# Reading a weight matrix as the moving matmul operand in runs of 8 tokens instead of single strided tokens or a reordered copy

## The chip, the cores and the metric

One core of one Trainium2 chip. The metric is the device time of one execution in microseconds (us), the median of several runs. In this kernel TensorE (PE in the profile) multiplies matrices: one operand, `lhsT`, is loaded first (PEld in the profile, whose page counts 4826 loads for 4826 matmuls), the other, `rhs`, is the moving operand. Operands lie in the memory called SBUF, results in the one called PSUM. VectorE (DVE) and ScalarE (ACT) move results out of PSUM, GpSimd (POOL) prepares the next batch and issues loads.

## The reference

The input `x` is 8 batches of 3008 tokens with 256 features. A two-dimensional Fourier transform is followed by an MLP-mixer block:

```python
X = np.fft.fft(np.fft.fft(x, axis=1), axis=2)
x = X.real
xt = x.transpose(0, 2, 1)
h = np.maximum(xt @ w_tok1, 0.0) @ w_tok2          # w_tok2: 256 x 3008
u = x + h.transpose(0, 2, 1)                       # "the add into u"
h2 = np.maximum(u @ w_ch1, 0.0) @ w_ch2            # 256 -> 1536 -> 256
return u + h2
```

The change touches only the second product of the token mixer, `... @ w_tok2` ("tok2"), and the add into `u`.

## The kernel before: the parts that matter

The kernel factors 3008 as 64 x 47: token `t = 47*b + a`. The Fourier tables leave the tokens of `u` ordered "k2-major": all 64 values of `b` for the first `a`, then for the next `a`, and so on. `w_tok2` lies in SBUF (`w2s`, 16-bit floats) in natural order, so tokens that are neighbours in k2-major order lie 47 elements, or 94 bytes, apart.

The token axis is cut in six chunks of 512 columns (eight `a`, the last one seven: 448 columns). For each chunk and each half `h` of the features, two matmuls add into one PSUM tile `pu`, and DVE adds `yt`, the Fourier part:

```python
w2p = const.tile([P, 2, S], FP16, tag="w2p")

def w2_cols(c):
    a0, a1 = 8 * c, min(8 * c + 8, NQ)                       # NQ = 47
    return w2s[:].rearrange("p h (b a) -> p h a b", a=NQ)[:, :, a0:a1, :]

def order_w2(c, th):                                         # ACT makes the copy
    a0, a1 = 8 * c, min(8 * c + 8, NQ)
    out_ = w2p[:, th, 64 * a0:64 * a1].rearrange("p (a b) -> p a b", b=64)
    copy(0, out_, w2_cols(c)[:, th])
# ... (in the generator `front(b)`, which makes u of batch b) ...
for c in range(NCH):                                         # 6 chunks
    f0 = CW * c
    n = min(CW, S - f0)
    for h in range(2):
        pu = ps_f("pu")                                      # PSUM, 3 buffers
        for th in range(2):
            nc.tensor.matmul(pu[:, 0:n], lhsT=uu[:, th, int(minus), h, :],
                             rhs=(w2_cols(c)[:, th] if b == 0 else
                                  w2p[:, th, f0:f0 + n]), ...)
        # ... y = the piece of yt, forwards or mirrored ...
        nc.vector.tensor_tensor(out=ut[:, h, f0:f0 + n], in0=pu[:, 0:n],
                                in1=y, op=AT.add)
```

Batch 0 cannot wait for the copy and reads `w2s` with the stride. In batch 0 ACT also makes the copy `w2p`, which batches 1 to 7 read contiguously. The rest of TensorE's work is the channel mixer: `pc` (`u @ w_ch1`) and `po` (`@ w_ch2`). `front(b+1)` is woven between the `pc` and `po` groups of batch `b`.

## Time and profile before

Median 672.84 us of 3 runs (672.61 to 676.21).

| | before |
|---|---|
| PE busy, share of the span | 647.4 us, 96% |
| DVE / ACT busy | 333.5 / 327.5 us |
| 24 tok2 matmuls of batch 0 (stride of 94 bytes), 512 columns | 1409 ns each |
| 168 tok2 matmuls of batches 1 to 7 (contiguous), 512 columns | 379 ns each |
| first tok2 matmul of batch 0 / of batch 1 / last of batch 7 | 41.1 / 137.4 / 596.1 us |

First the page: busy time by engine, and the chain of work that ended last.

```profile
span 672.3 us, 11899 instructions
PE 647.4 (96%) x4826; PEld 431.8 (64%) x4826; DVE 333.5 (50%) x726; ACT 327.5 (49%) x671; POOL 244.6 (36%) x242
...
PE 93%; POOL 2%; DVE 2%; ACT 2%; issue 1%; DVEq 0%; POOLq 0%; ACTq 0%
```

TensorE is the limit. The windows view gives, for each stretch of time, the busy time of PE, PEld (the weight loads), DVE, ACT and POOL, then the granted TensorE clock, the share of DMA time and GB/s:

```profile
40.00:60.00 20.00, 18.90 (x38) 4.56 (x38) 7.76 (x14) 5.10 (x9) 12.15 (x10) 0.66 0.53 113
225.00:300.00 75.00, 75.00 (x590) 52.13 (x588) 38.03 (x82) 37.06 (x81) 31.24 (x27) 1.00 0.46 85
```

In the steady part TensorE has no idle time at all, so what is added to a matmul is paid. Early in batch 0 its granted clock is 0.66, two thirds of full.

The groups by line and form, for tok2 and its two companions (the columns: busy us, mean ns of one | idle time of the engine before them, and what ended it):

```profile
L509 DVE TENSOR_TENSOR ut<-pu,yt 128x512 f16<-128x512 f32 x80 | 52.3, 680 | 44.6 <-PE pu L500 44.6
L500 PE MATMUL pu<-w2p,uu 128*128 128x512 f16 x140 | 37.8, 379 | 0.2 <-DVE ut L509 0.2
L500 PE MATMUL pu<-w2s,uu 128*128 128x512 f16 x20 | 26.0, 1409 | 0.3 <-ACT qs L485 0.3
L291 ACT ACTIVATE w2p<-w2s 128x512 f16<-128x512 f16 x10 | 14.3, 1433 | 0.0
```

The tile view of tok2 has the first and last starts:

```profile
L500 PE MATMUL pu<-w2s,uu x24: 1232/1402/1424, 41.1 to 125.5; 128*128 128x512 f16 x20, 128*128 128x448 f16 x4
L500 PE MATMUL pu<-w2p,uu x168: 350/379/379, 137.4 to 596.1; 128*128 128x512 f16 x140, 128*128 128x448 f16 x28
```

A matmul's mean is its duration from start to end; in a row, they overlap (contiguous ones are 379 ns long and start 215 ns apart). The cost is the distance from one start to the next. The timeline of PE shows it (start, length, then the instructions that were merged):

```profile
70.06 2.62 PE L500 MATMUL pu<-w2s,uu 128*128 128x512 f16 x2
72.48 1.49 PE L532 MATMUL pc<-ut,wc1p 128*128 128x512 f16 x6
...
106.99 2.76 PE L532 MATMUL pc<-ut,wc1m 128*128 128x512 f16 x6
...
211.12 0.59 PE L500 MATMUL pu<-w2p,uu 128*128 128x512 f16 x2
211.55 1.30 PE L532 MATMUL pc<-ut,wc1m 128*128 128x448 f16 x6
```

Two strided matmuls hold TensorE from 70.06 to 72.48: 1.21 us each, about 2.4 ns a column. Two contiguous ones hold it from 211.12 to 211.55: 0.215 us each. At 106.99, six `pc` matmuls take nearly twice their usual time (2.76 us, where six take 1.49 at 72.48): the granted clock has fallen to half again (0.50 from 107.0 to 109.7 us, 1.00 from 70.0 to 72.5).

### The profile page before, as it was taken

The numbers are of one execution on the slowest core, as the hardware profiler recorded it, in microseconds if no ns is written. First come the engines' busy times: TensorE is split into PE (matmuls) and PEld (weight loads), VectorE is DVE, ScalarE is ACT, GpSimd is POOL, SyncE is SP. The second block draws the span as 40 slices with busy tenths as digits, with TensorE's granted clock in tenths as the row PEclk, the third lists the DMA queues.
The fourth block names the chain that finished last, engine by engine and source line by source line (L and its number), as shares of the span: only waits on it lengthen the run. The fifth ranks groups of instructions, "written<-read, shape, count | busy, mean of one in ns | idle before, by whom it ended". The sixth has DMA issues, their size and how long they took to land.

```text
span 672.3 us, 11899 instructions
## 1 busy us (share of the span) xinstructions
PE 647.4 (96%) x4826; PEld 431.8 (64%) x4826; DVE 333.5 (50%) x726; ACT 327.5 (49%) x671; POOL 244.6 (36%) x242
## 2 busy tenths in 40 slices
PE   4789999999999999999999999999999999999996
PEld 3533454666776767667766677666766677666665
DVE  8743332473366435654366435653366435654342
ACT  6625674426553565336543555346553655334341
POOL 8829729624930096204930096205800000000000
PEclk9878998999999999999999999999999999999999
DMA  9991541734292235725292336622241332232432
GB/s 154 172 193 35 100 96 39 99 82 71 48 155 68 64 81 101 100 55 85 55 166 50 63 91 107 85 70 68 48 92 35 63 91 48 48 79 60 95 78 60
DMA packets 86486, 56.27 MB, mean 84 GB/s; under 512 B 54768, under 2 KB 83376, under 8 KB 85680
## 3 DMA queue, kind: packets, MB, share of 16 engines
q1 hardware_dynamic: 78176, 38.04, 27.4%
q0 software_dynamic: 8256, 17.49, 16.4%
q8 instruction: 37, 0.61, 0.4%
q14 instruction: 17, 0.14, 0.1%
HBM read 34.98 MB, written 24.64 MB: 89 GB/s over the span
## 4 chain that ended last, share of the span: by engine, by line
PE 93%; POOL 2%; DVE 2%; ACT 2%; issue 1%; DVEq 0%; POOLq 0%; ACTq 0%
PE po L551 37%; PE pc L532 37%; PE pu L500 9%; PE pw L443 2%; PE pz L416 1%; PE pw L444 1%; PE py L482 1%; PE pq L482 1%; DVE ut L509 0%; ACT uu L474 0%; PE pz L432 0%; PE ph L363 0%; DVE osb L565 0%; POOL xm L118 0%; PE pz L426 0%
## 5 line engine op out<-in xcount | busy, mean ns | idle before, releaser
L532 PE MATMUL pc<-ut,wc1p 128*128 128x512 f16 x576 | 143.3, 385 | 0.4 <-DVE ut L509 0.4
L532 PE MATMUL pc<-ut,wc1m 128*128 128x512 f16 (+1 forms) x576 | 136.2, 373 | 0.0
L565 DVE TENSOR_TENSOR osb<-po,rt 128x254 f32<-128x254 f32 (+6 forms) x264 | 77.2, 346 | 59.1 <-PE po L551 54.7
L532 PEld LDWEIGHTS <-wc1p 128*128 128x128 f16 x576 | 53.9, 99 | 65.2 <-issue 20.0
L399 POOL TENSOR_TENSOR eo<-xp 94x512 f16<-94x512 f16 (+1 forms) x28 | 33.9, 1211 | 165.3 <-PE pz L432 164.1
L532 PEld LDWEIGHTS <-wc1m 128*128 128x128 f16 x576 | 55.1, 98 | 54.4 <-issue 1.1
L509 DVE TENSOR_TENSOR ut<-pu,yt 128x512 f16<-128x512 f32 (+1 forms) x96 | 61.6, 670 | 56.4 <-PE pu L500 56.4
L394 POOL TENSOR_TENSOR xd<-xp,xm 94x1024 f16<-94x1024 f16 x28 | 59.3, 2119 | 64.4 <-DMA xm<-in_x_dram,ix_76 64.4
L395 POOL TENSOR_TENSOR xp<-xp,xm 94x1024 f16<-94x1024 f16 x28 | 59.3, 2120 | 2.2
L291 ACT ACTIVATE w<-pw 128x259 f16<-128x259 f32 x90 | 30.1, 386 | 53.3 <-PE pw L444 52.7
L291 ACT ACTIVATE z<-pz 128x480 f16<-128x480 f32 (+1 forms) x59 | 34.3, 662 | 26.3 <-PE pz L416 19.4
L500 PE MATMUL pu<-w2p,uu 128*128 128x512 f16 (+1 forms) x168 | 44.2, 375 | 0.5 <-DVE ut L509 0.5
L487 DVE TENSOR_TENSOR yt<-py,qs 128x512 f16<-128x512 f32 x48 | 30.6, 686 | 19.5 <-ACT qs L485 9.7
L403 POOL TENSOR_TENSOR eo<-xd 94x508 f16<-94x508 f16 (+1 forms) x28 | 33.7, 1203 | 0.0
L500 PE MATMUL pu<-w2s,uu 128*128 128x512 f16 (+1 forms) x24 | 30.7, 1383 | 0.3 <-ACT qs L485 0.3
L500 PEld LDWEIGHTS <-uu 128*128 128x128 f16 x192 | 19.0, 99 | 13.1 <-issue 4.4
L485 ACT ACTIVATE qs<-pq 128x512 f32<-128x512 f32 x24 | 14.1, 596 | 19.4 <-PE pq L482 8.9
L443 PE MATMUL pw<-td_305,z 128*128 128x259 f16 x96 | 21.7, 277 | 0.9 <-ACT w L291 0.6
L444 PE MATMUL pw<-td_304,z 128*128 128x131 f16 x96 | 19.0, 223 | 0.0
L474 ACT ACTIVATE uu<-uv 128x256 f16<-128x256 f32 (+2 forms) x48 | 13.2, 337 | 9.9 <-DVE uv L469 9.9
L128 POOL DMA_DIRECT2D xp<-in_x_dram x32 | 17.2, 560 | 0.2 <-issue 0.2
L118 POOL DMA_INDIRECT xm<-in_x_dram,ix_76 x16 | 15.3, 955 | 4.7 <-issue 4.6
(420 smaller groups left out, 1136.8 us busy)
## 6 DMA issues: line engine op xcount, KB each, us to landing
out_dram<-osb SPq DMA_DIRECT2D x88, 256.0 KB, 3.3
xp<-in_x_dram POOLq DMA_DIRECT2D x16, 272.0 KB
xp<-in_x_dram POOLq DMA_DIRECT2D x16, 127.5 KB
rt<-ut SPq DMA_TRANSPOSE x96, 3.3
out_dram<-osb SPq DMA_DIRECT2D x8, 192.0 KB, 3.2
w2s<-in_moe_w_tok_dram POOLq DMA_DIRECT2D x1, 1504.0 KB
w1p<-in_moe_w_tok_dram POOLq DMA_DIRECT2D x2, 384.0 KB
wc_148<-in_moe_w_ch_dram POOLq DMA_DIRECT2D x1, 768.0 KB
```

Source lines behind the costliest of these rows:

```text
L291: nc.scalar.activation(out=out_, in_=in_, func=AFT.Copy)
L394: eng.tensor_tensor(out=xd[:, t, :], in0=xp[:, t, :], in1=rv, op=AT.subtract)
L395: eng.tensor_tensor(out=xp[:, t, :], in0=xp[:, t, :], in1=rv, op=AT.add)
L399: eng.tensor_tensor(out=eo[:, t, 1:129], in0=xp[:, t, 1:129], in1=xp[:, t, 255:127:-1], op=AT.add)
L403: eng.tensor_tensor(out=eo[:, t, 129:256], in0=xd[:, t, 1:128], in1=xd[:, t, 255:128:-1], op=AT.subtract)
L443: nc.tensor.matmul(pw[:, 0:WD], lhsT=zb, rhs=td1[:], start=True, stop=False)
L487: nc.vector.tensor_tensor(out=yt[:, h, CW * c:CW * c + CW], in0=py[:], in1=qs[:], op=op)
L500: nc.tensor.matmul(pu[:, 0:n], lhsT=uu[:, th, int(minus), h, :], rhs=(w2_cols(c)[:, th] if b == 0 else w2p[:, th, f0:f0 + n]), start=(th = ...
L509: nc.vector.tensor_tensor(out=ut[:, h, f0:f0 + n], in0=pu[:, 0:n], in1=y, op=AT.add)
L532: nc.tensor.matmul(pc[:, 0:n], lhsT=wc[:, h, ct * P:(ct + 1) * P], rhs=ut[:, h, f0:f0 + n], start=(h == 0), stop=(h == 1))
L551: nc.tensor.matmul(po[0:n, o:o + D], lhsT=c1[:, ct, ks * P:ks * P + n], rhs=wc2[:, ct, :], start=(ct == 0), stop=(ct == NCT - 1))
L565: nc.vector.tensor_tensor(out=osb[r, ks_, j], in0=src[r, k0:k1, j], in1=rt[r, ks_, p], op=AT.add)
```

## The change

The intent: read `w2s` as it lies, but eight neighbouring tokens at a time (for every `b`, the eight `a` of the chunk, 16 bytes). PSUM then holds the columns b-major, and the DVE add, which reads PSUM anyway, turns them to k2-major by its access pattern. All batches do the same; the copy and its 12 ACT instructions go.

```diff
-    w2p = const.tile([P, 2, S], FP16, tag="w2p")
-
     def w2_cols(c):
         a0, a1 = 8 * c, min(8 * c + 8, NQ)
-        return w2s[:].rearrange("p h (b a) -> p h a b", a=NQ)[:, :, a0:a1, :]
-
-    def order_w2(c, th):
-        ... (the copy by ACT)
+        return w2s[:].rearrange("p h (b a) -> p h b a", a=NQ)[:, :, :, a0:a1]
@@ front(b)
-                                     rhs=(w2_cols(c)[:, th] if b == 0 else
-                                          w2p[:, th, f0:f0 + n]),
+                                     rhs=w2_cols(c)[:, th],
@@
-                nc.vector.tensor_tensor(out=ut[:, h, f0:f0 + n], in0=pu[:, 0:n],
-                                        in1=y, op=AT.add)
+                nc.vector.tensor_tensor(
+                    out=ut[:, h, f0:f0 + n].rearrange("p (a b) -> p a b", b=64),
+                    in0=pu[:, 0:n].rearrange("p (b a) -> p a b", b=64),
+                    in1=y.rearrange("p (a b) -> p a b", b=64), op=AT.add)
@@ the main loop, batch 0
-                    if 3 <= sub < 15:
-                        order_w2((sub - 3) // 2, (sub - 3) % 2)
```

More of the change, by code (lines that the diff above doesn't have):

```diff
@@ L368, in carried @@
                  ph[:])
-    w2p = const.tile([P, 2, S], FP16, tag="w2p")
     def w2_cols(c):
         a0, a1 = 8 * c, min(8 * c + 8, NQ)
-        return w2s[:].rearrange("p h (b a) -> p h a b", a=NQ)[:, :, a0:a1, :]
-    def order_w2(c, th):
-        a0, a1 = 8 * c, min(8 * c + 8, NQ)
-        out_ = w2p[:, th, 64 * a0:64 * a1].rearrange("p (a b) -> p a b", b=64)
-        copy(0, out_, w2_cols(c)[:, th])
+        return w2s[:].rearrange("p h (b a) -> p h b a", a=NQ)[:, :, :, a0:a1]
     state = {}
```

## The prediction

For reading it: a *line* is a stretch of 16 bytes that starts at a multiple of 16, a *visit* the reading of the columns that lie in one line, a *crossing* a run's passing from one line to the next. The trace of before does not show this length; the author assumed it, with a tile that starts on a line, and e4 and e6 measured it later. In the estimate, 2.40 ns is the column of the strided pairs above, and 0.42 ns that of contiguous matmuls in a row (0.215 us for 512).

> **What bounds it now.** TensorE. The page gives PE 647.4 of 672.3 us (96%); 93% of the chain of waits is PE. In the windows from 150 to 600 us PE is busy 75.00 of 75 us at full granted clock, DVE 38, ACT 37. A nanosecond added to a matmul there is paid in full; DVE and ACT work is nearly free.
>
> **tok2 now.** By form, 24 matmuls of batch 0 read w2s with a stride of 94 bytes: 1409 ns (512 columns). In the chain of waits pairs take 2.46 us: 2.40 ns a column. The 168 of batches 1 to 7 read the contiguous copy: 379 ns each, but in a row the timeline shows about 0.22 us each (8 in 1.80 us). Batch 0 thus pays 24 x 1.0 = 24 us for stride. ACT's 17 us for the copy are hidden (PE waits of about 1 us in batch 0). The window 40:60 has a granted clock of 0.66, and the timeline shows half-speed matmuls after strided ones (six pc in 2.56, not 1.30 us, at 107 us): about 4 us more.
>
> **After.** All 192 read runs of 8 halves (16 bytes), one every 94 bytes. [...] Seven of eight runs straddle two lines (94 is 14 modulo 16; tile start assumed aligned): 15 line visits per 64 columns instead of 8. [...] My estimate: a visit costs the larger of 2.40 ns and 0.42 ns x columns taken. That is 38 ns per 64 columns, 304 ns per matmul in a row[...]. I take 297.
>
> - Batches 1 to 7: 168 x about +79 ns (the last chunk is shorter) = +13 us, all critical.
> - Batch 0: 24 x about -0.91 us = -21 us, critical.
> - Clock and ACT in batch 0: -3.5 us; about 1.5 given back, since after the first four pu PE must wait for two DVE adds of 0.69 us, and POOL's fold of batch 1 (ends 75.3 us) gets close to its use (90.5 us now, about 76 after).
> - DVE add: PSUM read with step 8 floats. DVE's CAST z<-pz with step 96 took 680 ns for 480 elements, where a contiguous 512 took 692; so 680 to 720 ns, no effect.
>
> Sum: about -11 us.
>
> **Prediction: 662 us, 8 in 10 between 648 and 677.** Faster by over 2%: 0.38; within 2%: 0.54; slower: 0.08. Break-even is a spacing of about 355 ns per matmul; 2% faster needs below about 290, 2% slower above about 430.
>
> **What shows it.** By form: one group pu<-w2s x192, mean 450 to 470 ns for 512 columns. PE in a steady 75 us window stays 75.00; each of batches 1 to 7 gets 1.9 us longer (period now about 75.05 us). Batch 0 (first pu at 41.1 to last at 125.5 us) gets over 20 us shorter, with a granted clock over 0.8 in 40:60. ACT falls by 17 us. DVE add within 5%.
>
> **What would make it wrong.** (1) The run price: if only single-column visits cost, 645 to 653; if every break in the address stalls besides the crossing, 670 to 690. (2) A DVE read of PSUM with step 8 much dearer (over 1 us): PE waits for pu buffers when several pu come together. (3) New waits on POOL or the x loads eating batch 0's gain.

The sum came to about -11 us from +13, -21, -3.5 and +1.5 (rounded as they stand, they add to -10). The first two rest on 297 ns a matmul, an estimate.

## The result

656.83 us, the median of 4 runs (655.34 to 657.53), against 672.85 us (before, now with a fourth run): ratio 0.9747, 95% interval 0.9718 to 0.9777. That is faster by 2.5%. A ratio here is the mean time of one kernel's fast runs over that of the other's of the same rounds, so it is not quite the ratio of the medians.

The page after:

```profile
span 655.1 us, 11887 instructions
PE 630.6 (96%) x4826; PEld 429.4 (66%) x4826; DVE 333.4 (51%) x726; ACT 312.2 (48%) x659; POOL 244.4 (37%) x242
...
PE 92%; POOL 3%; DMA 2%; DVE 1%; issue 1%; ACT 0%; DVEq 0%; POOLq 0%
```

TensorE is still the limit, with 17 us less work; ACT lost 15 us. The windows after:

```profile
40.00:60.00 20.00, 18.43 (x86) 8.76 (x86) 11.26 (x20) 8.41 (x15) 11.92 (x8) 0.83 0.57 127
225.00:300.00 75.00, 75.00 (x579) 50.99 (x577) 37.54 (x82) 37.05 (x80) 30.09 (x27) 1.00 0.46 85
```

In 40:60 TensorE has 86 matmuls instead of 38, at a granted clock of 0.83 instead of 0.66. In the steady window it has 579 instead of 590. The groups after:

```profile
L501 DVE TENSOR_TENSOR ut<-pu,yt 128x512 f16<-128x512 f32 x80 | 52.2, 679 | 28.6 <-PE pu L493 28.5
L493 PE MATMUL pu<-w2s,uu 128*128 128x512 f16 x160 | 51.5, 429 | 0.3 <-ACT qs L478 0.3
```

The turning add takes 679 ns, where the plain one took 680. A run-reading matmul takes 429 ns, between 379 and 1409. The timeline after:

```profile
60.66 0.69 PE L493 MATMUL pu<-w2s,uu 128*128 128x512 f16 x2
61.19 1.46 PE L526 MATMUL pc<-ut,wc1p 128*128 128x512 f16 x6
```

A pair holds TensorE from 60.66 to 61.19 (0.525 us before rounding): 0.262 us each. So a run-reading matmul costs 47 ns more than a contiguous one and about 950 ns less than a strided one.

Three time marks of the two traces (first and last starts in the tile views; the first tok2 of batch 1 after the change is at 113.1 us) split the whole difference of the spans (672.3 - 655.1 = 17.2 us):

```profile
L493 PE MATMUL pu<-w2s,uu x192: 398/425/632, 41.1 to 578.9; 128*128 128x512 f16 x160, 128*128 128x448 f16 x32
```

| stretch | before | after | difference |
|---|---|---|---|
| start to first tok2 of batch 0 | 41.1 us | 41.1 us | 0.0 |
| from there to first tok2 of batch 1 | 96.3 us | 72.0 us | -24.3 |
| from there to last tok2 of batch 7 | 458.7 us | 465.8 us | +7.1 |
| from there to the end | 76.2 us | 76.2 us | 0.0 |

Batch 0 won 24.3 us; batches 1 to 7 gave back 7.1. Within batch 0, the pairs of strided matmuls shrank from 2.43 to 0.525 us (512 columns, ten pairs) and from 2.12 to 0.47 us (448 columns, two pairs), at full clock: about 22.3 us together. The other 2.0 us are clock and waits: by the distances from start to start, the other matmuls of batch 0 lost about 5.3 us to half clock before and 2.2 after, and about 1.2 us came back, in a longer wait for the first adds and in tok2 matmuls that now ran at half clock. (The strided ones lost nothing to it: 1.19 to 1.23 us each at either clock, as the four from 41.13 to 46.01 us at a mean granted clock of 0.55 and the two from 70.06 to 72.48 at 1.00.)

### The profile page after: what moved, and what is told of

The parts are those of the page before. It is cut to its first block, busy times and chain, and to the rows that moved or that the text cites. A ratio compares the mean times of both kernels' runs of the same rounds, so it can differ in the third digit from the quotient of the medians.

```text
span 655.1 us, 11887 instructions
## 1 busy us (share of the span) xinstructions
PE 630.6 (96%) x4826; PEld 429.4 (66%) x4826; DVE 333.4 (51%) x726; ACT 312.2 (48%) x659; POOL 244.4 (37%) x242
## 4 chain that ended last, share of the span: by engine, by line
PE 92%; POOL 3%; DMA 2%; DVE 1%; issue 1%; ACT 0%; DVEq 0%; POOLq 0%
PE po L545 39%; PE pc L526 38%; PE pu L493 7%; DMA xp<-in_x_dram 2%; PE pw L436 1%; PE pz L409 1%; PE pw L437 1%; PE py L475 1%; PE pq L475 1%; PE pz L425 0%; POOL xm L118 0%; POOL w1p L140 0%; PE pz L419 0%; POOL w1m L140 0%; POOL gr L231 0%
## 5 line engine op out<-in xcount | busy, mean ns | idle before, releaser
L526 PE MATMUL pc<-ut,wc1m 128*128 128x512 f16 (+1 forms) x576 | 134.8, 370 | 0.0
L493 PE MATMUL pu<-w2s,uu 128*128 128x512 f16 (+1 forms) x192 | 60.5, 424 | 0.3 <-ACT qs L478 0.3
L128 POOL DMA_DIRECT2D xp<-in_x_dram x32 | 17.2, 558 | 0.2 <-issue 0.2
L118 POOL DMA_INDIRECT xm<-in_x_dram,ix_76 x16 | 15.3, 954 | 4.7 <-issue 4.6
L409 PE MATMUL pz<-t1n,eo 94*128 94x96 f16 x240 | 14.3, 207 | 1.9 <-DVE z L289 1.5
```

Source lines behind the costliest of these rows:

```text
L526: nc.tensor.matmul(pc[:, 0:n], lhsT=wc[:, h, ct * P:(ct + 1) * P], rhs=ut[:, h, f0:f0 + n], start=(h == 0), stop=(h == 1))
```

## The experiments

Two theories of the gain were tested. T1: only the reads matter, with the split above. T2: part of it comes from freeing ACT of its copies. A second question was why a run costs 47 ns a matmul where the prediction had about 80.

### e0: the changed kernel again

No edit; the yardstick for e1 to e3, on the same chip.

> The changed kernel once more, as the yardstick of this chip for the three below. Expected 655 to 658 us, ratio to before 0.975, since its four runs so far lie between 655.3 and 657.5.

Measured: 656.33 us (655.27 to 657.15), ratio 0.9718. As before.

### e1: runs in batch 0, contiguous copy later

```diff
+    w2p, order_w2 and its calls as before the change
-                                     rhs=w2_cols(c)[:, th],
+                                     rhs=(w2_cols(c)[:, th] if b == 0 else
+                                          w2p[:, th, f0:f0 + n]),
+                if b == 0: (the turning add)
+                else:      (the plain add)
```

> Batch 0 reads w2s in runs of 8 as the change does; ACT makes the k2-major copy again and batches 1 to 7 read it contiguously with the plain add, as before the change. Theory T1 (the gain is the strided reads of batch 0, and batches 1 to 7 pay 0.047 us for each of 168 run reads): 656.8 - 7.7 = about 649 us, faster than both. Rival T2 (a part of the gain, up to 3 us, comes from freeing ACT of its 17 us of copies in batch 0): about 652 us. The first theory of the price of runs put in the prediction (0.08 us a matmul) would say 644.

Measured: 649.09 us (648.25 to 650.07), ratio 0.9616. Against e0 this is -7.2 us; from the first tok2 of batch 1 to the last of batch 7 it takes 458.7 us again:

```profile
L500 PE MATMUL pu<-w2p,uu x168: 349/379/379, 112.0 to 570.7; 128*128 128x512 f16 x140, 128*128 128x448 f16 x28
```

That is T1's number, and a kernel faster than both.

### e2: the copies made and not read

```diff
+    w2p, order_w2 and its calls as before the change (nobody reads w2p)
```

> The changed kernel, but ACT still makes the 12 copies of w_tok2 in batch 0 and nobody reads them. T1: ACT is off the chain, so the time is that of the changed kernel, within 0.7 us (ratio to it 1.000). T2: 2 to 3 us longer, about 659 us. The copies should be shorter or longer than 1.43 us only by what their reads cost: they still write k2-major.

Measured: 655.43 us (654.91 to 657.92), ratio 0.9707; that is 0.9 us less than e0, where T2 had 2 to 3 us more. The copies took 1437 ns each, as before:

```profile
L291 ACT ACTIVATE w2p<-w2s 128x512 f16<-128x512 f16 x10 | 14.4, 1437 | 0.0
```

No gain from removing ACT's copies shows beside the spread of the runs (about 2 to 3 us in each kernel, medians 0.9 us apart the other way). T2, as put down, falls.

### e3: later batches in runs that are aligned to 16 bytes

```diff
+    w2q = const.tile([P, 2, 64, 48], FP16, tag="w2q")        # rows of 47 padded to 48
+    def order_w2(c, th):                                      # called as before the change
+        copy(0, w2q[:, th, :, a0:a1], w2_cols(c)[:, th])
-                                     rhs=w2_cols(c)[:, th],
+                                     rhs=(w2_cols(c)[:, th] if b == 0 else
+                                          w2q[:, th, :, 8 * c:8 * c + n // 64]),
```

> Batch 0 as in the changed kernel; batches 1 to 7 read a copy of w_tok2 whose rows of 47 tokens are padded to 48 halves (96 bytes), so every run of 8 starts on a 16-byte boundary and fills one line. The add still turns the columns. If the price of a run is that of crossing lines (54 more line visits per matmul, 0.84 ns each) or of visits of a single column, matmuls are spaced 0.216 us apart and the time is about 649 us, as with the contiguous copy. If every break in the address costs 0.73 ns, spacing stays at 0.262 us and the time at about 657 us.

Measured: 650.51 us (648.59 to 651.52), ratio 0.9629. The groups of tok2 matmuls and of the copy, by form:

```profile
L499 PE MATMUL pu<-w2q,uu 128*128 128x512 f16 x140 | 37.8, 379 | 0.2 <-DVE ut L508 0.2
L499 PE MATMUL pu<-w2q,uu 128*128 128x448 f16 x28 | 7.3, 379 | 0.2 <-DVE ut L508 0.2
L291 ACT ACTIVATE w2q<-w2s 128x512 f16<-128x512 f16 x10 | 6.4, 636 | 0.0
```

Still 64 runs a matmul, with a break in the address after each, and 379 ns, the time of a contiguous read. The six chunks start 0 to 5 whole lines into a row, and the durations of all 168 lie between 376 and 379 ns. So breaks are free for whole lines, and the 47 ns are a matter of alignment; e4 tests this with the pitch held fixed. Turning in the add is free here too (a median of 681 ns for the adds). Runs of 7 columns (the last chunk) take 379 ns as well, not 352 as in the contiguous copy; 28 x 27 ns = 0.8 us, which is the 0.7 us by which e3's batches 1 to 7 (459.4 us) are longer than e1's. The cheaper copy (636 instead of about 1435 ns) gains nothing that shows, as e2 leads one to expect.

### e4: a price list of reading patterns

After the last output, groups of 24 matmuls (12 for the two dearest) in a row, each with one pattern of the moving operand; the output stays right. The run was a single one, so its state (fast or slow) is unknown; its total is of no interest.

```diff
+    def priced(name, rhs, count=24, n=512):
+        pm = ps_out(name)
+        for _ in range(count):
+            nc.tensor.matmul(pm[:, 0:n], lhsT=ident[:], rhs=rhs, start=True, stop=True)
+    def runs(s, k=8, pitch=48):          # wf: w2s as one flat row
+        return wf[:, s:s + 64 * pitch].rearrange("p (b a) -> p b a", a=pitch)[:, :, 0:k]
+    priced("line", wf[:, 0:512])
+    for s in range(8):
+        priced("run%d" % s, runs(s))
+    priced("run47", runs(0, 8, 47)); ... runs of 7, step 2, 4, contiguous, step 8, contiguous, stride 47, contiguous
```

> The changed kernel with groups of matmuls after its last output, 24 in a row over one pattern of the moving operand (w2s taken as a flat row; the time of the whole is of no interest, the output stays right). 512 columns each: contiguous, expected 0.216 us apart; runs of 8 every 96 bytes, starting 0 to 7 halves past a 16-byte boundary; runs of 8 and of 7 every 94 bytes, expected 0.262 and 0.235 us as in the kernel; steps of 2, 4, 8 halves, and the stride of 94 bytes, expected 1.23 us. Price by single-column visits: starts 1 and 7 at 0.40 us, all others at 0.216. Price by line crossing: start 0 at 0.216, starts 1 to 7 all at 0.27. Price by break: all eight at 0.262. The prediction's rule (2.40 ns a visit at least): start 0 at 0.216, starts 1 and 7 at 0.34, starts 2 to 6 at 0.31; steps 2 and 4 at 0.31 and 0.62. [...] After the strided groups the contiguous ones should start at half clock (0.43 us)[...].

Measured, as the mean distance from start to start in the trace (ns per matmul of 512 columns; for step 8 and the stride the steady value, since the first of a group is up to 40 ns shorter). A half is one 16-bit number:

| pattern | ns |
|---|---|
| contiguous | 216 |
| runs of 8 every 96 bytes, start 0 / 1 / 2 / 3 halves past a line | 216 / 303 / 267 / 269 |
| start 4 / 5 / 6 / 7 | 231 / 269 / 248 / 269 |
| runs of 8 every 94 bytes (the kernel's) | 260 |
| runs of 7 every 94 bytes (448 columns) | 234 |
| step 2 (four columns a line) | 226 |
| step 4 (two columns a line) | 451 |
| step 8 (one column a line, neighbouring lines) | 900 |
| stride of 94 bytes | 1233 |

The profile's own view of one tile shows the same order by duration (min/median/max in ns; in time, starts 0, 1, 2, 4 and 6, then the runs of 94 bytes; a duration here is its distance plus about 163 ns):

```profile
L634 PE MATMUL run<-w2s,ident x21: 379/379/379, 659.0 to 663.3; 128*128 128x512 f16 x21
L634 PE MATMUL run<-w2s,ident x23: 463/466/468, 664.0 to 670.6; 128*128 128x512 f16 x23
L634 PE MATMUL run<-w2s,ident x23: 431/431/432, 671.2 to 677.1; 128*128 128x512 f16 x23
L634 PE MATMUL run<-w2s,ident x22: 392/393/393, 684.3 to 689.2; 128*128 128x512 f16 x22
L634 PE MATMUL run<-w2s,ident x22: 410/412/415, 696.4 to 701.6; 128*128 128x512 f16 x22
L634 PE MATMUL run<-w2s,ident x22: 422/422/422, 708.8 to 714.2; 128*128 128x512 f16 x22
```

None of the four price rules that stand as rivals in the expectation fits as it stood. The price by break falls at start 0 (216); the price by single columns falls at starts 2, 3 and 5; the price per crossing falls because starts 1 to 7 differ (231 to 303). The prediction's rule, that a visit to a line costs the larger of a fixed time and 0.42 ns a column, falls with its 2.40 ns, but fits the steps, and runs on average, once its constant is read from the neighbouring lines of the list: 900 / 512 = 1.76 ns. This constant was chosen after the fact, from step 8; the rest follows from it. Step 2 visits 256 / 2 = 128 lines, and 128 x 1.76 = 225 ns (measured 226); step 4 visits 256, which gives 451 (451). Split runs: with 216 / 512 = 0.42 ns a column, start 4 gives 64 x 2 x 1.76 = 225 (231), start 1 gives 64 x (7 x 0.42 + 1.76) = 302 (303), and the mean over the eight starts is 261, where the mean of the measured is 259 and the kernel's pattern has 260. (94 bytes is no multiple of 16, and the kernel's 64 runs go through all eight starts in turn, so the mean of the starts is the fair comparison; it holds without any rule.) Single starts stray from the rule by up to 33 ns (start 7: 302 by the rule, 269 measured; start 3: 248 and 269), and so do the aligned runs of 7 of e3 (189 by the rule, 215 from start to start), which stays unexplained.

The end of the list answers for the clock. The contiguous group ahead of the strided ones ran at 216 ns, but these are contiguous matmuls just after the group of step 8 and after that of 94 bytes, by the view of one tile:

```profile
L634 PE MATMUL backb<-w2s,ident x7: 631/631/631, 753.4 to 756.0; 128*128 128x512 f16 x7
L634 PE MATMUL backc<-w2s,ident x8: 380/631/631, 775.5 to 778.4; 128*128 128x512 f16 x8
```

The windows view of the same stretches (granted clock 0.50):

```profile
753.00:756.00 3.00, 3.00 (x9) 1.04 (x8) 0.00 (x0) 0.00 (x0) 0.00 (x0) 0.50 0.00 0
776.00:778.00 2.00, 2.00 (x6) 0.68 (x5) 0.00 (x0) 0.00 (x0) 0.00 (x0) 0.50 0.00 0
```

631 instead of 379 ns, 427 ns apart: half clock. TensorE never lacked an instruction here (PE is busy in all of both windows), and yet after columns at 1.8 to 2.4 ns each the granted clock was 0.50; what the clock follows, no trace shows. By the granted clocks of windows, spells of half clock that end within a trace lasted about 3.4 us (before, 100 to 110 us: 0.83), 6.8 (after, 41 to 50 us: 0.62), 10 (e4, 740 to 760 us: 0.74), 13.7 (before, 41 to 50 and 50 to 60 us: 0.53 and 0.74) and 17.1 us (e5, 30 to 41, 41 to 50 and 50 to 60 us: 0.94, 0.50 and 0.66). The groups of runs, and those of step 2 and step 4, kept full clock (1.00 in the windows within them).

### e5: the halves of the change exchanged

```diff
-                                     rhs=w2_cols(c)[:, th],
+                                     rhs=(w2_cols(c)[:, th].rearrange("p b a -> p a b")
+                                          if b == 0 else w2_cols(c)[:, th]),
+                if b > 0: (the turning add)
+                else:     (the plain add)
```

> The two halves of the change exchanged: batch 0 reads w2s with the 94-byte stride and the plain add, as before the change; batches 1 to 7 read runs of 8 with the turning add; no copy. T1: batch 0 keeps its 24 us, batches 1 to 7 pay 7.7 us, so 672.8 + 7.7 = about 680 us, ratio 1.011. T2: up to 3 us less, since ACT is freed of the copies, about 677. With the prediction's price for runs it would be 686.

Measured: 683.28 us (679.44 to 684.65), ratio 1.0135 (1.0102 to 1.0168), against before at 673.62: the same within 2%, and 3 us above T1's number. Its span is 9.2 us longer than the first trace of before. From the first tok2 of batch 1 (139.5 us) to the last of batch 7 (605.3) it takes 465.8 us, exactly as the changed kernel: +7.1. The other 2.1 us lie in batch 0, where this trace has 23.9 us at half clock from 39.8 us on, where that of before has 17.1. A gain from freeing ACT of the copies does not show here either, though one of up to about 2 us could hide behind the clock; e2 is the test of it.

### e6: one column a line, by pitch

The changed kernel with a second list of 12 matmuls each, 64 columns at a fixed pitch, then the next 64 one half further.

```diff
+    for pitch in (8, 16, 24, 32, 40, 46, 47, 48, 49, 56, 64, 80):
+        priced("pitch%d" % pitch,
+               wf[:, 0:64 * pitch].rearrange("p (b a) -> p a b", a=pitch)[:, 0:8, :])
```

> The changed kernel with another list after its last output: 12 matmuls of 512 columns each, every column in another 16-byte line than the one before: 64 columns at a fixed pitch, then the next 64 one half further. Pitches of 8, 16, 24, 32, 40, 48, 56, 64, 80 halves are 1 to 8 and 10 whole lines, 46, 47, 49 lie between. The first list had 1.76 ns a column for neighbouring lines and 2.41 for a pitch of 47 halves. If distance sets the price, every pitch but 8 is near 2.41; if the price follows which lines collide, it varies with the pitch (some near 1.76, powers of two dearer); if it is the pitch of no whole lines, only 46, 47 and 49 differ from 1.76.

A single run again, its state unknown. Measured from start to start in the trace, ns a column: pitch 8: 1.75, 16: 1.79, 24: 1.73, 32: 1.67, 40: 2.08, 46: 2.40, 47: 2.41, 48: 2.50, 49: 2.15, 56: 1.81, 64: 1.68, 80: 1.95. The price is neither that of distance (64 halves cost less than 8) nor of pitches that are no whole lines (48, six lines, is the dearest), and the whole multiples of 32 are the cheapest, not the dearest. It varies with the pitch between 1.67 and 2.50 ns, so the kernel's stride of 47 happens to be among the dear ones. Why is open. The clock is not the reason: it was 1.00 up to 657.1 us and 0.50 from there to the end of the list (the mean of the whole run is 0.908), and the matmuls of pitch 8 are 900 ns apart on both sides. That TensorE stayed at half clock for all of these 140 us, with no gap between its matmuls (144 in 147.2 us by the timeline), shows again what e4 showed: reads of one column a line, at 1.67 to 2.50 ns each, went with half clock though TensorE always had work.

### e7 and e8: TensorE kept warm in batch 0

"Warm" means at full clock. e7 is e1 with small matmuls whose result nobody reads (`filler`, a helper that the kernel already has), where TensorE waits for the first `u` of batch 0; e8 is e1 again, on the same chip.

```diff
                     nc.vector.tensor_tensor(out=yt[:, h, CW * c:CW * c + CW], in0=py[:], in1=qs[:], op=op)
+            if b == 0:
+                filler(8)
             yield
@@ after the two matmuls into pu
+                if b == 0 and c == 0 and h == 1:
+                    filler(12)
```

> As e1 (batch 0 in runs, contiguous copy later), with small idle-work matmuls (8 after each of batch 0's three table steps, 12 after the first four pu) where TensorE waits between 36 and 44 us, so that it doesn't fall to half clock then. If the half clock left in batch 0 (6.8 us in the changed kernel after 45 us) comes from those waits, it goes, and the time falls by 1 to 2.5 us against e1; if it comes from the reads in runs, it stays and the time is that of e1 or up to 1 us longer.

> e1 once more, as the yardstick for e7 on this chip: 648 to 650 us.

Measured: e7 647.95 us (647.52 to 648.79), ratio 0.9615; e8 649.54 us (647.86 to 650.06), ratio 0.9631. The windows view for 41 to 50 us, first of e7, then of e8:

```profile
41.00:50.00 9.00, 8.37 (x47) 3.85 (x45) 6.16 (x11) 3.89 (x8) 2.00 (x1) 1.00 0.81 181
```

```profile
41.00:50.00 9.00, 7.87 (x22) 2.74 (x22) 5.00 (x10) 2.68 (x6) 1.15 (x1) 0.62 0.87 188
```

The clock is 1.00 instead of 0.62, so what half clock the run-reading kernels had left came from the waits before, not from their reads. The gain of 1.6 us between the medians is within what was expected, but the ranges of the runs overlap and the intervals of the ratios overlap: the clock is shown, the gain is likely.

## Why the prediction was right, and what in it was off

- **The limit.** Right. TensorE's steady windows stayed at 75.00 of 75 us, and the time moved as the sum of its matmuls did.
- **Batch 0, -21 us for the reads and -2.0 for the rest.** Right, and in its parts too: the trace has about -22.3 and -2.0 (clock about -3, given back about 1.2). The clock in 40:60 rose to 0.83, as forecast (over 0.8). The wait for the first adds of batch 0 grew from 0.35 to 0.86 us; nothing waited for POOL.
- **ACT.** Counted in "-3.5 us, clock and ACT". Its part did not show: e2 put the copies back and lost no time. ACT's busy time fell by 15.3 us, where 17 was forecast.
- **The DVE add.** Right: 679 ns forecast as 680 to 720, and e3 shows the same.
- **Batches 1 to 7, +13 us.** The mis-sized term: 168 x 79 ns was put down, 7.1 us was measured, so 1.0 us a batch instead of 1.9. (At 47 ns each it would be 7.9; before the change two tok2 matmuls waited 0.5 us in all for an add, and after it none did.) The failed step is "a visit costs the larger of 2.40 ns and 0.42 ns x columns taken". The form of the rule held on average, though not for single starts (e4); the constant was read from the only strided read in the trace, and the stride of 47 has a dear pitch (e6: 2.41 ns a column, against 1.75 at pitch 8). With the 1.76 ns of neighbouring lines (e4), the rule gives 261 ns, and the kernel has 262. The prediction forecast a mean of 450 to 470 ns for 512 columns, and the trace has 429.
- **The sum.** -11 forecast, -16 measured (medians; -17.2 between the spans). 656.83 lies within 648 to 677. The class was forecast with 0.38 for faster and 0.54 for within 2%; the class it held likeliest did not come: the mis-sized term, 6 us of 673, is all of the difference.

Not shown: why single starts of a run, and aligned runs of 7, stray from the rule, and why the price of a scattered column depends on the pitch as it does.

## What to carry to other kernels

As a first estimate, cost a strided moving operand by the 16-byte lines it visits, with a constant measured for that pitch: here, against 216 ns for a contiguous matmul, four columns a line were nearly free (226), two cost double (451), one cost four to six times as much (1.67 to 2.50 ns a column in e6, 855 to 1280 ns), and runs of a whole line were free if aligned (216) and cost a fifth more if not (260). Read in runs where the data is used once or early, and let the engine that empties PSUM turn the columns, which cost nothing here (679 against 680 ns an add); keep a contiguous copy where it is read often and an idle engine can make it (with ACT's copies put back, e2 took 655.43 us against 656.33). The best kernel was neither of the two: runs in batch 0, the copy in the other seven (649.09 us), and a little less with TensorE kept warm (647.95 us).
